# High words of queries and keys by ScalarE casts in place of transfers, in a clustered attention with two MLPs

## The chip, the cores and the metric

The kernel runs on one core of a Trainium2 chip. The metric is the device time of one execution in microseconds. Engines are named as in the profile: TensorE (PE, with PEld for its weight loads), VectorE (DVE), ScalarE (ACT), GpSimd (POOL) and SyncE (SP), whose queue issues nearly all the transfers (DMAs).

## The reference

Each query and each key is assigned to the nearest of 16 centroids of its head, and a query attends only to keys of its own cluster. The result goes through two MLPs, the second of them gated.

```python
batch, n_heads, seq, head_dim = (2, 8, 768, 64)          # 16 heads in all
q_assign = np.argmax(np.einsum('bhsd,hcd->bhsc', q_n, c_n), axis=-1)
k_assign = np.argmax(np.einsum('bhsd,hcd->bhsc', k_n, c_n), axis=-1)
mask = q_assign[:, :, :, None] == k_assign[:, :, None, :]
scores = np.where(mask, scale * np.matmul(q, k.transpose(0, 1, 3, 2)), -1000000000.0)
attn = np.exp(scores - np.max(scores, axis=-1, keepdims=True))
attn = attn / (np.sum(attn, axis=-1, keepdims=True) + 1e-09)
x = np.matmul(attn, v)          # then (1536, 512) rows
h = x @ w_in                    # 512 x 2048
x = (h * (1.0 / (1.0 + np.exp(-1.702 * h)))) @ w_out
g = x @ w_gate                  # 512 x 1536
out = (g * (1.0 / (1.0 + np.exp(-g))) * (x @ w_val)) @ w_out2
```

## The kernel before

**Attention** goes head by head (h = 0 to 15). A head has two stages on TensorE. In the *scores* stage twelve steps (six blocks of keys times two halves of 384 queries) each issue two matmuls into a bank `st` of PSUM (L707; three banks in turn), and beside each step one matmul `smax` of the *next* head (L657), whose maximum VectorE takes (`nm`, L662). ScalarE turns each `st` into exponentials `p` (L717). In the *values* stage TensorE multiplies `p` by v (`pv`) and sums of `p` by ones (`ps`, both L739); ScalarE needs no scores there, and does what is prepared for later heads.

**Low and high words.** TensorE reads 32-bit words in a rounded form, so queries and keys are split in a high word (rounded) and a low word (the rest). `q2` and `k2` of a head have 128 partitions and two planes: plane 0 of q2 has the high queries in rows 0 to 63 and the low ones in rows 64 to 127, plane 0 of k2 the low keys and then the high keys; plane 1 has the high words in rows 0 to 63, then 16 rows of the cluster and the row of maxima. For heads 8 to 15 the raw queries and keys lie together in one of four staging tiles `st` (q in rows 0 to 63, k in rows 64 to 127; `load_qk`, L428). `hi_staged` (L461) casts the whole of it into plane 0 of q2; so the high keys stand for a while where the low queries belong. `spread_hi` has three transfers (L468): the high keys from there to both planes of k2, and the high queries to plane 1 of q2. `lo_staged` (L465, VectorE) subtracts the high words from the staging tile, in place, and `spread_lo` (two transfers, L468 too) puts the low words in q2 and k2.

**Similarities.** At the end of the scores of an odd head h, `similar` computes the similarities to the centroids of heads h + 3 and h + 4 (`sims`, L572, eight matmuls), which need the high and low words of both; VectorE turns them into assignments (`largest`, then `assign` in the next, even head: `T`, `mx`, `oT`, two casts on ScalarE and two transfers from `oT`, L642 and L644). `mrow` (L689, after the first values) and the cast L691 make the row of maxima of head h + 1.

**Decoding.** The MLPs' weights arrive as 64-bit numbers. A piece is fetched raw (L265), ScalarE takes it apart (`a`, L280 and `t`, L283), VectorE joins it (L286, then L291 to `wo`), and it is stored (`keep`, L300 or L302). Six pieces are decoded in attention; `takes` says at which head and which block c of the values each part is done: part 0 is ScalarE's, parts 1 and 2 are VectorE's. Pool `dec` has one tile for each of `a` and `t`.

**The end of attention and the MLPs** are ordered by a planner (`Plan`): tasks with an estimated time, dependencies and a latest start taken from TensorE's order, which is fixed by the order in which tasks are made. The last head's scores are tasks of that plan, between the first products of the MLP. `late_from` says from which tile on a ring (a set of tiles used in turn) lies in memory that attention held.

Each engine and the SP queue run their instructions in order: an instruction that waits holds all behind it.

Of the kernel before, what the change touches and what calls it, by code (L numbers as in the profile page):

```python
# [184 lines left out]
def tile_cluster_attention_two_mlps(ctx: ExitStack, tc: tile.TileContext, qk, v, cen, w1, w2, wg, wv, w3, out):  # L185
    nc = tc.nc
# [16 lines left out]
    def pool(stack, name, bufs, **kw):  # L203
        return stack.enter_context(tc.tile_pool(name=name, bufs=bufs, reuse_waits="tile", **kw))
# [5 lines left out]
    xc_p = [pool(ctx, "xc0", X0)]  # L210
    xf_p = [pool(ctx, "xf0", 1)]
    raw_p = pool(ctx, "raw", RAW - 1)
    dec_p = pool(ctx, "dec", 1)
    wo_p = pool(ctx, "wo", 1)
    r_p = [pool(ctx, "r0", 1)]
    scr_p = pool(ctx, "scr", 1, space=DRAM)
    ps_m = pool(ctx, "ps_m", 1, space=PSUM)
# [241 lines left out]
    def hi_staged(h):  # L459

        nc.scalar.copy(q2(h)[:, 0, :], stage[h % NST])  # L461

    def lo_staged(h):
        t = stage[h % NST]
        nc.vector.tensor_tensor(out=t.bitcast(F32R), in0=t, in1=q2(h)[:, 0, :].bitcast(F32), op=ALU.subtract)  # L465

    def bits(to, of):
        nc.sync.dma_start(out=to.bitcast(F32), in_=of.bitcast(F32))  # L468

    def spread_hi(h):  # L470
        bits(k2(h)[D:2 * D, 0, :], q2(h)[D:2 * D, 0, :])
        bits(k2(h)[0:D, 1, :], q2(h)[D:2 * D, 0, :])
        bits(q2(h)[0:D, 1, :], q2(h)[0:D, 0, :])

    def spread_lo(h):
        bits(q2(h)[D:2 * D, 0, :], stage[h % NST][0:D])
# [375 lines left out]

    takes = {}
    for h in range(5, 5 + EARLY_ITEMS, 2):
        takes.update({(h, 0): (0,), (h, 1): (1, 2), (h, 3): (0,), (h, 5): (1,), (h + 1, 4): (2,)})
    sims = similar([0])
    keep_warm(18)
    hi_k(1)
# [145 lines left out]
    for h in range(NH):  # L1004
# [11 lines left out]
        if h == NH - 1:  # L1016
            moved_sums(h - 1)
            send_sums(h - 1)
        if h > 2:
            moved(h - 1)  # L1020
            if h % 2 and 4 < h < NH - 1:
                load_sums((h - 3) // 2)
# [9 lines left out]
        if 1 < h < NH - 1:  # L1032
            mneg(h + 1)
            if h % 2 and ahead and h > 3:
                do(largest([h + 3, h + 4], similar([h + 3, h + 4], ps_s, "s")))
            for part in takes.get((h, 0), ()):
                take(part)
            values(h, 0)
            values(h, 1)
            mrow(h + 1)  # L1040
        if h > 1 and h + 2 < NH:
            load_v(h + 2)
        if h + 6 < NH and h > 1:
            load_qk(h + 6)
        casts = [] if not h else [h + 4] if h < 3 else [7, 8] if h == 3 else [h + 5] if h + 5 < NH else []
        if h > 3 and casts:
            hi_staged(casts[0])
        elif casts and h != 1:
            hi_q(casts[0])
            hi_k(casts[0])  # L1050
        elif casts:
            hi_q(casts[0])
# [13 lines left out]
        for c in range(SC) if more else ():  # L1066
            if h > 1:
                if c > 1:
                    values(h, c)
                beside_block(h, c)  # L1070
            elif h or c:
                pv(h, c)
            if c == 0:
                if h < 2:
                    load_v(h + 1)
                    if h:
                        load_v(h + 2)
                        hi_k(casts[0])
                    for i in casts:
                        lo_q(i, nc.gpsimd)  # L1080
                        lo_k(i, nc.gpsimd)
                    load_qk(h + 6)
                if ahead:
                    if h + 5 == NH:
                        close_slot(FIRST)
                        close_slot("st")
                        xs_p.append(right("xs", 2))
                        xc_p.append(right("xc1", XC - X0 - 1))
            if h == 0:
# [12 lines left out]
            if h == 1:  # L1102
                beside(2, c, ((ps_m, "m"), (ps_s, "s")))
                if c == 3:
                    mneg(2)
                    sims = similar([4], ps_s, "s")
                    mrow(2)
                if c == 4:
                    do(largest([4, 5], sims + similar([5], ps_s, "s")))
            for part in takes.get((h, c), ()) if c else ():  # L1110
                take(part)
            for i in casts[-1:] if h > 2 else ():
                for at, step in ((2, spread_hi), (2, lo_staged), (5, spread_lo)):
                    if c == at and h > 3:
                        step(i)
            if h in (2, 3) and c == 1:
                lo_q(casts[0])
                lo_k(casts[0])
            for n in beside_values.get((h, c), ()):
                next(more_steps[n], None)  # L1120
            if h == 1 and c == 4:
                fetch_to(2)
            if h == 3 and c == 4:
                do(largest([6, 7], similar([6, 7], ps_s, "s")))
                hi_staged(8)
                spread_hi(8)
            if h == 4 and c == 1:
                lo_staged(8)
                spread_lo(8)
            if h == 3 and c in (3, 4):  # L1130
                to_x(0, c - 3)
# [9 lines left out]
    def after_attention():  # L1141
        close_slot((NH - 1) % NQK)
        slot_stack["c"].close()
        att.close()
        late_pools.update(
            {n: pool(ctx, f"{n}_late", bufs) for n, bufs in (
                ("c", CB // 2), ("e", EB - 1), ("wd", WO), ("g", GB), ("xc", 1), ("sp", 3), ("b0", 1), ("w", 1), ("raw", 1), ("dec", 1), ("wo", 1),
            )},
            a=pool(ctx, "ps_a", 1, space=PSUM),
        )  # L1150
# [14 lines left out]
    a_tile, t_tile, wo_tile = (in_turn((lambda pl=pl: pl, 1), (lambda n=n: late(n), 1)) for pl, n in ((dec_p, "dec"), (dec_p, "dec"), (wo_p, "wo")))  # L1165
    rings = {
        "raw": p.ring(RAW, lambda: raw_tile([128, 512, 2], I32, "raw")),
        "a": p.ring(2, lambda: a_tile([128, 512], F32, "a")), "t": p.ring(2, lambda: t_tile([128, 512], I32, "t")),
        "wo": p.ring(2, lambda: wo_tile([128, 512], F32, "wo")),
        "wd": p.ring(WO, late_tile("wd", [128, 512], F32, "wd")),  # L1170
        "w": p.ring(WB, new_wf, held["w"]),
        "s": p.ring(1, new_s, held["s"]),
        "b0": p.ring(2, lambda: new_block(0), held["b0"]),
# [16 lines left out]
    late_from.update({"a": 1, "t": 1, "wo": 1, "raw": RAW - 1, "w": WB - 1, "b0": 1, "xc": XC - 1, "c": CB // 2, "p1": 1, "u2": 1, "u3": 1})  # L1190

    kept = {}

# [389 lines left out]
    def last_values():  # L1583
        for c in range(SC):
            p.task(
                "PE", (2 + 2 * (c in SUMS)) * (2 * HALF / 2.4 + 5), lambda c=c: values(NH - 1, c), (), (),
                exp_tasks[2 * c:2 * c + 2] + [t for a in SUMS.get(c, ()) for t in adds[a]],
            )
            yield

# [3 lines left out]
    next(more)  # L1594
    next(first)
    next(more)
    last_adds()
    slots = last_values()
    for k in range(2):
# [10 lines left out]

    def plan_norm(hp, first):
        if hp > NH // 2 - 3:
            if first:
                first = [p.task("SP", 1000, lambda: send_sums(NH - 1), (), (), first)]
            got = p.task("SP", 1000, lambda: load_sums(hp), (), (), first)
            turned = p.task("DVE", 350, lambda: invert(hp), (), (), [got])
            first = [p.task("SP", 1000, lambda: (send_recips(hp), load_recips(hp)), (), (), [turned, *norms[:-1]])]
        norms.append(p.task(
            "POOL", 1850, lambda: norm_pair(hp), (), [(last_x, (hp % (H // 2), t0)) for t0, _ in parts], first,
        ))  # L1620
        return norms[-1]

# [79 lines left out]
```

## Time and profile before

| | |
|---|---|
| median of 3 runs | 788.19 us (787.99 to 788.4) |
| the profiled execution | 790.38 us, span 788.6 us |
| granted TensorE clock, mean | 0.993 |
| PE busy | 773.5 us (98%) |
| DVE busy | 667.4 us (85%) |
| ACT busy | 485.4 us (62%) |
| POOL busy | 126.7 us (16%) |

All times in the rows are microseconds from the span's start, unless they say ns. Attention takes about the first 260 us, the two MLPs the rest. A busy TensorE is not one at its full clock: the granted clock is read beside it (1.00 is 2.4 GHz, 0.50 is 1.2 GHz). In rows of a timeline, the bracket at the end is the idle time of the engine ahead of the instruction, and what ended it.

### The profile page before, as it was taken

To read this page: it belongs to the slowest core of one execution; us is meant where nothing else is said; L and a number is where in the kernel's file an instruction comes from. 1 tells how busy PE (TensorE), PEld (TensorE's weight loads), DVE (VectorE), ACT (ScalarE), POOL (GpSimd) and SP (SyncE) were. 2 spreads that over 40 slices of the span, in tenths; PEclk is the share of its full clock that TensorE was granted. 3 is DMA by queue.
4 is the path that set the end of the run, shared out by engine and by line. 5 is a ranking of instruction groups with operands and counts; after the bars stand their busy time and mean duration, and the time that the engine had idled before them with its cause. 6 is when DMAs were issued, how large, how long until landed. Compare 5 with 4: busy or idle time off the path is not lost.

```text
span 788.6 us, 11966 instructions
## 1 busy us (share of the span) xinstructions
PE 773.5 (98%) x4238; PEld 662.6 (84%) x4238; DVE 667.4 (85%) x1220; ACT 485.4 (62%) x851; POOL 126.7 (16%) x136
## 2 busy tenths in 40 slices
PE   8999998989999999999999999999999999999998
PEld 6995766567575899999999999999999999999996
DVE  7887878879895899999799889999988998877752
ACT  7758656558576786787487767667453654534332
POOL 8564334335355000000000000000000000000000
PEclk9999999999999999999999999999999999999999
DMA  5132466555124477663166784647423222322102
GB/s 124 38 100 58 101 175 164 150 143 141 24 61 133 176 245 239 205 200 134 41 221 233 239 276 151 227 163 243 161 92 105 81 65 97 115 72 73 63 1 80
DMA packets 54427, 106.66 MB, mean 135 GB/s; under 512 B 19984, under 2 KB 25472, under 8 KB 54368
## 3 DMA queue, kind: packets, MB, share of 16 engines
q1 hardware_dynamic: 54144, 105.58, 43.1%
q8 instruction: 33, 0.54, 0.3%
q10 hardware_dynamic: 224, 0.33, 0.1%
q14 instruction: 26, 0.21, 0.1%
HBM read 76.23 MB, written 21.06 MB: 123 GB/s over the span
## 4 chain that ended last, share of the span: by engine, by line
PE 87%; DVE 8%; DMA 2%; issue 1%; ACT 1%; SPq 0%; DVEq 0%; ACTq 0%
PE h L384 36%; PE a L384 29%; PE pv L739 7%; PE st L707 6%; PE ps L739 3%; PE smax L657 3%; DVE nm L662 3%; PE pv L807 2%; DMA k<-st 1%; DMA k<-q 1%; PE sims L572 1%; DVE b L379 1%; PE warm L492 0%; DVE s L1246 0%; DVE wo L291 0%
## 5 line engine op out<-in xcount | busy, mean ns | idle before, releaser
L384 PE MATMUL h<-xc,b 128*128 128x384 f32 x1680 | 316.8, 337 | 0.1
L384 PEld LDWEIGHTS h<-xc,b 128*128 128x128 f32 x1680 | 291.7, 188 | 10.4 <-DVE u L1302 2.3
L384 PE MATMUL a<-g,sp 128*128 128x512 f32 (+1 forms) x768 | 144.3, 336 | 0.0
L384 PEld LDWEIGHTS a<-g,sp 128*128 128x128 f32 x768 | 124.9, 188 | 16.9
L384 PE MATMUL a<-sp,g 128*128 128x512 f32 x432 | 109.6, 393 | 0.0
L662 DVE TENSOR_REDUCE nm<-smax 128x1 f32<-128x384 f32 x192 | 98.6, 555 | 12.5 <-PE smax L657 12.0
L717 ACT ACTIVATE p<-st 128x384 f32<-128x384 f32 x192 | 88.5, 491 | 30.8 <-PE st L707 25.8
L726 POOL TENSOR_TENSOR add<-p 128x384 f32<-128x384 f32 x84 | 84.8, 1030 | 114.5 <-ACT p L717 112.9
L707 PE MATMUL st<-q,k 128*128 128x384 f32 (+1 forms) x384 | 97.9, 345 | 0.8 <-ACT p L717 0.8
L384 PEld LDWEIGHTS a<-sp,g 128*128 128x128 f32 x432 | 80.1, 187 | 13.2
L376 ACT CAST b<-s 128x512 fp32r<-128x512 f32 x80 | 49.5, 620 | 55.1 <-PE h L384 47.7
L707 PEld LDWEIGHTS st<-q,k 128*128 128x128 f32 (+1 forms) x384 | 68.2, 190 | 10.8 <-issue 7.2
L1302 DVE TENSOR_TENSOR u<-h,p 128x384 f32<-128x384 f32 x80 | 44.2, 553 | 30.3 <-PE h L384 30.1
L739 PE MATMUL pv<-p,v 128*64 128x384 f32 x336 | 69.2, 522 | 0.0
L657 PE MATMUL smax<-k,q 80*128 80x384 f32 x192 | 63.0, 345 | 1.2 <-DVE nm L662 0.8
L280 ACT ACTIVATE a<-raw 128x512 f32<-128x512 f32 x68 | 45.7, 672 | 23.0 <-DVE wo L291 10.6
L379 DVE TENSOR_TENSOR b<-s,b 128x512 fp32r<-128x512 f32 x80 | 54.7, 685 | 1.6 <-ACT b L376 0.4
L379 DVE TENSOR_TENSOR g<-c,g 128x768 fp32r<-128x768 f32 x56 | 52.6, 953 | 1.5 <-ACT g L376 0.9
L376 ACT CAST g<-c 128x768 fp32r<-128x768 f32 x56 | 45.3, 834 | 12.3 <-DVE c L1317 11.8
L286 DVE SCALAR_TENSOR_TENSOR t<-a,t 128x512 int32<-128x512 int32 x68 | 46.1, 683 | 3.9 <-ACT t L283 3.9
L376 ACT CAST b<-w 128x768 fp32r<-128x768 f32 x35 | 29.2, 834 | 29.7 <-PE h L384 29.7
L1310 ACT ACTIVATE c<-c 128x384 f32<-128x384 f32 (+1 forms) x56 | 38.3, 684 | 14.3 <-DVE c L1302 13.5
(141 smaller groups left out, 885.0 us busy)
## 6 DMA issues: line engine op xcount, KB each, us to landing
raw<-in_w SPq DMA_DIRECT2D x44, 512.0 KB, 3.9
w<-scr SPq DMA_DIRECT2D x30, 512.0 KB, 4.2
raw<-in_wg SPq DMA_DIRECT2D x12, 512.0 KB
raw<-in_wv SPq DMA_DIRECT2D x12, 512.0 KB, 3.9
w<-scrg SPq DMA_DIRECT2D x12, 512.0 KB, 4.0
w<-scrv SPq DMA_DIRECT2D x12, 512.0 KB, 3.5
st<-in_qk SPq DMA_DIRECT2D x31, 192.0 KB, 3.6
scr<-wd SPq DMA_DIRECT2D x23, 256.0 KB, 5.5
```

Source lines behind the costliest of these rows:

```text
L280: nc.scalar.activation(a, raw[:, :, 1].bitcast(F32), ACTF.Copy, scale=2.0**-112)
L286: nc.vector.scalar_tensor_tensor(out=t, in0=a.bitcast(I32), scalar=3, in1=t, op0=ALU.logical_shift_left, op1=ALU.bitwise_or)
L376: nc.scalar.copy(to, of)
L379: eng.tensor_tensor(out=to, in0=of, in1=hi.bitcast(F32), op=ALU.subtract)
L384: nc.tensor.matmul(out=out_ps, lhsT=lhs[a], rhs=rhs[b], start=(start and j == 0), stop=(stop and j == 2), skip_group_check=True, **kw)
L657: nc.tensor.matmul(out=ps, lhsT=q2(h)[0:ONE + NC, 1, c * 128:(c + 1) * 128], rhs=k2(h)[0:ONE + NC, 1, n * HALF:(n + 1) * HALF],)
L662: nc.vector.tensor_reduce(out=nm_t[h][:, c, n:n + 1], in_=ps, axis=AX.X, op=ALU.max)
L707: nc.tensor.matmul(out=ps, lhsT=k2(h)[0:rows, a, c * 128:(c + 1) * 128], rhs=q2(h)[0:rows, a, at], start=(a == 0), stop=(a == 1),)
L717: nc.scalar.activation(p_t[h, c][:, n * HALF:(n + 1) * HALF], ps, ACTF.Exp, scale=scale)
L726: nc.gpsimd.tensor_tensor(out=add_t[h, c][:, at], in0=p_t[h, c][:, at], in1=p_t[h, c + 1][:, at], op=ALU.add)
L739: nc.tensor.matmul(out=ps[n * D:(n + 1) * D, 0:HALF], lhsT=w, rhs=x[:, n * HALF:(n + 1) * HALF], start=start, stop=stop, skip_group_check= ...
L1302: lambda: nc.vector.tensor_tensor(out=to.tile[:, part], in0=ps.tile[:, 0:HALF], in1=other.tile, op=ALU.add),
```

## The change

1. `spread_hi` and its three transfers are gone. `hi_others` has three casts on ScalarE that take the high words straight from the staging tile: the high keys to both planes of k2, the high queries to plane 1 of q2.
2. `hi_staged` comes ahead of the values of a head, before the row of maxima; `hi_others` behind that row. `lo_staged` comes at block 1 of the values, `spread_lo` at block 2 (before: blocks 2 and 5). The fetches of v and of the next queries and keys come behind `spread_lo`; they stood ahead of the values' blocks.
3. The decoding parts move: in odd heads part 0 of the first piece from the start of the values to block 2, of the second to block 4; VectorE's parts behind `lo_staged`.
4. Pools `dec` and `wo` have two tiles from the start; before, the second lay in memory freed by attention.
5. In the last head, the copy of head 14's output (`moved`) becomes a task of the plan, and the sums of heads 12 and 13 are fetched at the head's start.

```diff
-    dec_p = pool(ctx, "dec", 1)
-    wo_p = pool(ctx, "wo", 1)
+    dec_p = pool(ctx, "dec", 2)
+    wo_p = pool(ctx, "wo", 2)
...
+    def hi_others(h):
+        nc.scalar.copy(k2(h)[D:2 * D, 0, :], stage[h % NST][D:2 * D])
+        nc.scalar.copy(k2(h)[0:D, 1, :], stage[h % NST][D:2 * D])
+        nc.scalar.copy(q2(h)[0:D, 1, :], stage[h % NST][0:D])
...
-    def spread_hi(h):
-        bits(k2(h)[D:2 * D, 0, :], q2(h)[D:2 * D, 0, :])
-        bits(k2(h)[0:D, 1, :], q2(h)[D:2 * D, 0, :])
-        bits(q2(h)[0:D, 1, :], q2(h)[0:D, 0, :])
...
-        takes.update({(h, 0): (0,), (h, 1): (1, 2), (h, 3): (0,), (h, 5): (1,), (h + 1, 4): (2,)})
+        takes.update({(h, 2): (0,), (h, 3): (1,), (h, 4): (0,), (h, 5): (2,), (h + 1, 3): (1, 2)})
...
         if h == NH - 1:
             moved_sums(h - 1)
             send_sums(h - 1)
-        if h > 2:
+            load_sums((h - 3) // 2)
+        elif h > 2:
             moved(h - 1)
...
-            for part in takes.get((h, 0), ()):
-                take(part)
+            if h > 3 and h + 5 < NH:
+                hi_staged(h + 5)
             values(h, 0)
             values(h, 1)
             mrow(h + 1)
-        if h > 1 and h + 2 < NH:
-            load_v(h + 2)
-        if h + 6 < NH and h > 1:
-            load_qk(h + 6)
...
         if h > 3 and casts:
-            hi_staged(casts[0])
+            hi_others(casts[0])
...
+            for i in casts[-1:] if h > 3 else ():
+                for at, step in ((1, lo_staged), (2, spread_lo)):
+                    if c == at:
+                        step(i)
+            if h > 1 and c == 2:
+                if h + 2 < NH:
+                    load_v(h + 2)
+                if h + 6 < NH:
+                    load_qk(h + 6)
+            for part in takes.get((h, c), ()):
                 take(part)
-            for i in casts[-1:] if h > 2 else ():
-                for at, step in ((2, spread_hi), (2, lo_staged), (5, spread_lo)):
-                    if c == at and h > 3:
-                        step(i)
...
-                spread_hi(8)
+                hi_others(8)
...
-    late_from.update({"a": 1, "t": 1, "wo": 1, "raw": RAW - 1, ...
+    late_from.update({"raw": RAW - 1, ...
...
+    moves = p.task("ACT", 2 * act(HALF), lambda: moved(NH - 2), (), ())
```

TensorE's instructions stand in the same order in both kernels. ScalarE, from the copy of the output at the end of the scores of head 5 (`xf<-pv`) to the first exponentials of head 6, before:

```order
L766 COPY xf<-pv 64x384 x2
L280 ACTIVATE a<-raw 128x512
L283 ACTIVATE t<-raw 128x512
L691 CAST row<-mrow 6x128
L461 CAST q_0_165<-st_196 128x768
L280 ACTIVATE a<-raw 128x512
L283 ACTIVATE t<-raw 128x512
L717 ACTIVATE p<-st 128x384 x5
```

And after:

```order
L766 COPY xf<-pv 64x384 x2
L461 CAST q_0_165<-st_196 128x768
L691 CAST row<-mrow 6x128
L464 CAST k_0_166<-st_196 64x768
L465 CAST k_0_166<-st_196 64x768
L466 CAST q_0_165<-st_196 64x768
L280 ACTIVATE a<-raw 128x512
L283 ACTIVATE t<-raw 128x512
L280 ACTIVATE a<-raw 128x512
L283 ACTIVATE t<-raw 128x512
L717 ACTIVATE p<-st 128x384 x5
```

The first cast now stands ahead of the row of maxima, three more behind it, and both decoding pairs behind these.

The SP queue in head 6, from the transfer of the row of maxima to the low words of head 11 (q_1, k_1), before:

```order
L692 DMA q_2_180<-row 1x6x128
L436 DMA v_192<-in_v 128x6x64
L428 DMA st_194<-in_qk 64x768 x2
L644 DMA q_4_170<-oT 16x768
L644 DMA k_4_171<-oT 16x768
L793 DMA r<-recips 64x768 x2
L468 DMA k_1_189<-q_1_188 64x768 x2
L468 DMA q_1_188<-q_1_188 64x768
L300 DMA scr_95<-wo 128x256 x2
L468 DMA q_1_188<-st_197 64x768
L468 DMA k_1_189<-st_197 64x768
```

And after, to the store of the decoded piece:

```order
L692 DMA q_2_180<-row 1x6x128
L644 DMA q_4_170<-oT 16x768
L644 DMA k_4_171<-oT 16x768
L793 DMA r<-recips 64x768 x2
L473 DMA q_1_188<-st_197 64x768
L473 DMA k_1_189<-st_197 64x768
L436 DMA v_192<-in_v 128x6x64
L428 DMA st_194<-in_qk 64x768 x2
L300 DMA scr_95<-wo 128x256 x2
```

The three transfers of high words are gone, and the low words passed the fetches and the store.

ScalarE at the start of the last head, where the sums of head 14 are copied (`sums<-ps`); a piece of the difference:

```order
 L769 COPY sums<-ps 65x384
-L766 COPY xf<-pv 64x384 x2
 L717 ACTIVATE p<-st 128x384 x6
-L1323 COPY p_3031<-h 128x384
+L766 COPY xf<-pv 64x384 x2
+L1322 COPY p_3038<-h 128x384
```

The copy of the output went from ahead of six exponentials to behind them.

## Rows read from the trace of the kernel before

**Rows 1.** Windows from values to values: length; PE, PEld, DVE, ACT, POOL busy; PEclk, DMA, GB/s.

```profile
88.83:119.87 31.04, 29.11 (x157) 19.24 (x158) 25.12 (x47) 19.72 (x41) 11.87 (x13) 0.95 0.63 161
119.87:150.95 31.08, 29.07 (x156) 19.20 (x158) 25.74 (x48) 19.72 (x41) 11.84 (x13) 0.95 0.64 165
150.95:198.07 47.12, 44.03 (x238) 29.45 (x239) 39.24 (x73) 31.25 (x63) 19.71 (x20) 0.96 0.54 134
198.07:210.89 12.82, 12.82 (x75) 8.80 (x77) 11.55 (x21) 6.60 (x15) 3.99 (x5) 1.00 0.08 18
```

**Rows 2.** Windows after the wait in head 7, and in the MLPs.

```profile
137.00:138.00 1.00, 1.00 (x6) 0.27 (x4) 0.93 (x3) 0.00 (x0) 0.00 (x0) 0.50 0.76 307
...
259.00:768.00 509.00, 508.90 (x2784) 472.49 (x2783) 450.43 (x795) 307.58 (x510) 1.84 (x1) 1.00 0.45 150
```

**Rows 3.** Timeline of TensorE: start, length, what [idle ahead, what ended it].

```profile
135.34 0.58 PE L572 MATMUL sims<-q,cs 128*128 128x384 f32 x2 [1.95 <-DMA q<-st]
...
190.94 0.45 PE L657 MATMUL smax<-k,q 80*128 80x384 f32 x1 [0.32 <-DVE nm L662]
...
195.32 0.34 PE L657 MATMUL smax<-k,q 80*128 80x384 f32 x1
195.49 0.52 PE L572 MATMUL sims<-q,cs 128*128 128x384 f32 x2
...
244.82 1.39 PE L707 MATMUL st<-q,k 128*128 128x384 f32 x6 [0.77 <-ACT p L717]
```

**Rows 4.** The chain that ended last, in head 7: start, length, what.

```profile
127.84 4.38 DMA k<-q
132.29 0.48 SPq L468
132.82 3.12 DMA k<-st
```

**Rows 5.** Timeline of ScalarE, from the end of head 7's scores.

```profile
132.93 0.95 ACT L766 COPY xf<-pv 64x384 f32<-64x384 f32 x2
133.90 0.67 ACT L280 ACTIVATE a<-raw 128x512 f32<-128x512 f32 x1
134.48 0.64 ACT L283 ACTIVATE t<-raw 128x512 int32<-128x512 uint32 x1
139.70 0.25 ACT L691 CAST row<-mrow 6x128 fp32r<-6x128 f32 x1 [4.58 <-PE mrow L689]
```

**Rows 6.** Timeline of ScalarE in the values of head 6.

```profile
121.50 0.25 ACT L691 CAST row<-mrow 6x128 fp32r<-6x128 f32 x1 [0.30 <-PE mrow L689]
121.66 0.82 ACT L461 CAST q<-st 128x768 fp32r<-128x768 f32 x1
123.95 0.83 ACT L642 CAST q<-oT 16x768 fp32r<-16x768 f32 x1 [1.47 <-DVE oT L630]
124.79 0.83 ACT L642 CAST k<-oT 16x768 fp32r<-16x768 f32 x1
126.71 0.49 ACT L717 ACTIVATE p<-st 128x384 f32<-128x384 f32 x1 [1.09 <-PE st L707]
```

**Rows 7.** Timeline of VectorE: the twelve maxima of heads 7 and 11.

```profile
126.89 6.38 DVE L662 TENSOR_REDUCE nm<-smax 128x1 f32<-128x384 f32 x12 [1.39 <-PE smax L657]
...
190.33 5.91 DVE L662 TENSOR_REDUCE nm<-smax 128x1 f32<-128x384 f32 x12
```

**Rows 8.** Groups by line over the span: times | busy us, mean ns | idle.

```profile
L286 DVE SCALAR_TENSOR_TENSOR t<-a,t 128x512 int32<-128x512 int32 x68 | 46.1, 683 | 3.9 <-ACT t L283 3.9
...
L465 DVE TENSOR_TENSOR st<-st,q 128x768 fp32r<-128x768 f32 x8 | 7.6, 956 | 0.1
...
L445 ACT CAST k<-st 64x768 fp32r<-64x768 f32 x7 | 5.8, 832 | 0.2
...
L785 DVE RECIPROCAL rc<-rc 128x12 f32<-128x12 f32 x7 | 1.6, 228 | 0.2
```

More of the change, by code (lines that the diff above doesn't have):

```diff
@@ L1109, in tile_cluster_attention_two_mlps @@
                     do(largest([4, 5], sims + similar([5], ps_s, "s")))
-            for part in takes.get((h, c), ()) if c else ():
+            for i in casts[-1:] if h > 3 else ():
[8 more added lines that the diff above has]
+            for part in takes.get((h, c), ()):
                 take(part)
-            for i in casts[-1:] if h > 2 else ():
-                for at, step in ((2, spread_hi), (2, lo_staged), (5, spread_lo)):
-                    if c == at and h > 3:
-                        step(i)
             if h in (2, 3) and c == 1:
@@ L1146, in after_attention @@
             {n: pool(ctx, f"{n}_late", bufs) for n, bufs in (
-                ("c", CB // 2), ("e", EB - 1), ("wd", WO), ("g", GB), ("xc", 1), ("sp", 3), ("b0", 1), ("w", 1), ("raw", 1), ("dec", 1), ("wo", 1),
+                ("c", CB // 2), ("e", EB - 1), ("wd", WO), ("g", GB), ("xc", 1), ("sp", 3), ("b0", 1), ("w", 1), ("raw", 1),
             )},
@@ L1164, in tile_cluster_attention_two_mlps @@
     raw_tile = in_turn((lambda: raw_p, RAW - 1), (lambda: late("raw"), 1))
-    a_tile, t_tile, wo_tile = (in_turn((lambda pl=pl: pl, 1), (lambda n=n: late(n), 1)) for pl, n in ((dec_p, "dec"), (dec_p, "dec"), (wo_p, "wo")))
     rings = {
         "raw": p.ring(RAW, lambda: raw_tile([128, 512, 2], I32, "raw")),
-        "a": p.ring(2, lambda: a_tile([128, 512], F32, "a")), "t": p.ring(2, lambda: t_tile([128, 512], I32, "t")),
-        "wo": p.ring(2, lambda: wo_tile([128, 512], F32, "wo")),
-        "wd": p.ring(WO, late_tile("wd", [128, 512], F32, "wd")),
+        "a": p.ring(2, new_a), "t": p.ring(2, new_t), "wo": p.ring(2, new_wo), "wd": p.ring(WO, late_tile("wd", [128, 512], F32, "wd")),
         "w": p.ring(WB, new_wf, held["w"]),
@@ L1189, in tile_cluster_attention_two_mlps @@
     late_from = {n: 0 for n in ["wd", "g", "sp"] + [f"acc{i}" for i in range(6)]}
-    late_from.update({"a": 1, "t": 1, "wo": 1, "raw": RAW - 1, "w": WB - 1, "b0": 1, "xc": XC - 1, "c": CB // 2, "p1": 1, "u2": 1, "u3": 1})
+    late_from.update({"raw": RAW - 1, "w": WB - 1, "b0": 1, "xc": XC - 1, "c": CB // 2, "p1": 1, "u2": 1, "u3": 1})
     kept = {}
@@ L1586, in last_values @@
                 "PE", (2 + 2 * (c in SUMS)) * (2 * HALF / 2.4 + 5), lambda c=c: values(NH - 1, c), (), (),
-                exp_tasks[2 * c:2 * c + 2] + [t for a in SUMS.get(c, ()) for t in adds[a]],
+                exp_tasks[2 * c:2 * c + 2] + [t for a in SUMS.get(c, ()) for t in adds[a]] + [moves],
             )
@@ L1612, in plan_norm @@
         if hp > NH // 2 - 3:
-            if first:
+            if hp == NH // 2 - 1:
                 first = [p.task("SP", 1000, lambda: send_sums(NH - 1), (), (), first)]
-            got = p.task("SP", 1000, lambda: load_sums(hp), (), (), first)
-            turned = p.task("DVE", 350, lambda: invert(hp), (), (), [got])
+                first = [p.task("SP", 1000, lambda: load_sums(hp), (), (), first)]
+            turned = p.task("DVE", 350, lambda: invert(hp), (), (), first)
             first = [p.task("SP", 1000, lambda: (send_recips(hp), load_recips(hp)), (), (), [turned, *norms[:-1]])]
         norms.append(p.task(
-            "POOL", 1850, lambda: norm_pair(hp), (), [(last_x, (hp % (H // 2), t0)) for t0, _ in parts], first,
+            "POOL", 1850, lambda: norm_pair(hp), (), [(last_x, (hp % (H // 2), t0)) for t0, _ in parts], [*first, moves],
         ))
```

## The prediction

> **What bounds the kernel now.** I read the windows first, then TensorE's timeline, then the chain of waits, then ScalarE and VectorE beside it. From 259 us on, TensorE is busy 508.90 of 509 us at the full clock [rows 2]: the two MLPs leave nothing to win, and the order of TensorE's instructions is the same in both kernels, so the change can act only in attention. There the undisturbed pace is known: a head without similarities takes 12.82 us, in which TensorE is busy 12.82 [rows 1]. Every odd head also runs eight matmuls of similarities; a matmul starts 0.17 after the one before it (the two rows at 195 in [rows 3]), so they add 8 x 0.175 = 1.4. A pair of heads should take 2 x 12.82 + 1.4 = 27.04. It takes 31.04 (heads 4 and 5) and 31.08 (6 and 7), and heads 8 to 10 take 47.12 where 3 x 12.82 + 2 x 1.4 = 41.26 would do [rows 1]. The excess is 4.00 + 4.04 + 5.86 = **13.9 us**, and that is the prize.
>
> Its cause stands in the chain [rows 4]. At the end of an odd head TensorE waits 1.95 us for the low words of the last head (at 135.34 in [rows 3]; there are three of this kind, and a shorter one at 196.7). Those words go into rows 64 to 127 of q2, from which the high words of the keys are first copied away by two transfers. So SP's queue holds the low transfer back until the high ones have landed (4.38 from issue), then spends 0.48 issuing q and 3.12 until k lands. After each of the three long waits TensorE works on at half clock: a microsecond in that stretch shows it busy 1.00 with a granted clock of 0.50, its lower level of 1.2 GHz (137 to 138 us in [rows 2]). This half of the loss is not in the idle time at all.
>
> The Trainium skill (Trainium Kernel Development and Optimization, Best Practices) says that matmul busy time is no measure of the distance to the limit. The trace agrees: 137 to 138 shows a busy engine at half its pace, and by idle time alone the three long waits, about 2 us each, would put the prize near 6 us.
>
> **The change part by part.** *The transfers of high words go*, 3 for each of 8 heads, and with them the wait between high and low. Three casts on ScalarE take their place. One such cast of 64 x 768 takes 0.832 [rows 8], so 2.5 us a head and 24 x 0.832 = 20.0 us in all. Nothing of that costs time if it lies under the values (the stage after the scores, where TensorE needs no exponentials). That has to be checked in an even and in an odd head.
>
> Even head (number 6, values from 119.87): ScalarE is done with the head before at 121.50 - 0.30 = 121.20 [rows 6]. Now follow the first cast 0.82 to 122.02, the row of maxima 0.25 to 122.27, three casts 2.5 to 124.8, the two casts of the assignment 1.7 to 126.5. The exponentials start at 126.71 after an idle 1.09. The cover holds with 0.2 to spare.
>
> Odd head (number 7), without the stall: the similarities follow the last scores and the values start about 133.9. ScalarE is done with the head before at 132.93 + 0.95 = 133.88 [rows 5]; first cast to 134.7; the row must wait for some nine matmuls, about 135.6, and ends at 135.85; casts to 138.35; then two decoding pairs, each 134.48 + 0.64 - 133.90 = 1.22, to 140.8. The exponentials are wanted 126.71 - 119.87 = 6.84 after the start of the values, at 140.76. That is even. Three banks of scores let TensorE run about 0.5 ahead (one step of a score takes 0.53, twelve in 6.38 [rows 7]), so a delay under 0.5 costs nothing. If ScalarE comes out later, the loss is what exceeds that 0.5.
>
> The Trainium skill (ScalarE: Activation LUTs, What ACT_TABLE_LOAD costs) gives 186 ns + 0.833 ns an element with 93 ns of overlap between neighbours. The duration agrees (0.826 against 0.832). The overlap shows at 121.50 to 121.66 and between the decoding steps, but the two casts at 123.95 and 124.79 show none. With it the three casts take an estimated 2.3, ScalarE is done 0.2 sooner, and rival B below would have a chance of one in ten.
>
> *VectorE's steps are the same, in another order.* The low step (0.956 [rows 8]) now waits until the casts have read the staging tile, since it overwrites it: to 138.35 in the odd head. Behind it are queued a decoding step 0.683, two short ones below 0.23, another 0.683: done about 141.1. The first maximum was wanted 126.89 - 119.87 = 7.02 after the start of the values [rows 7], at 140.94. So it is 0.15 late, and up to 0.5 if VectorE itself comes later to the low step. Twelve maxima back to back take 5.91 instead of 6.38 [rows 7], so it is made up within the scores. In the even head: 124.8 + 0.96 + 2 x 0.69 = 127.1 against 126.89; same verdict. Bounds: nothing to 0.5 a head over seven heads; I take 0.9 in all.
>
> *Low words.* In the even head the low step ends at 125.8. SP then has q and k to issue; k starts about 126.9 behind the transfers of the assignment and the reciprocals, and lands 3.12 to 4.38 later [rows 4], 130.0 to 131.3. The second similarities want it at 135.34 - 1.95 = 133.39 [rows 3]. Two microseconds to spare: the four waits go, and with them the half clock. What is late next is ScalarE or VectorE, as above. The fetches of v and of the next queries and keys move behind the low words on SP; they start to move about 4.5 us before the next head's first cast wants them, against 3.12 to 4.38 for transfers of that size [rows 4], and that cast may come 0.9 late before the row of maxima suffers. Raw weights queue behind them; nobody waits for those within a head.
>
> *Head 10* stays bound by VectorE: TensorE loses 0.32 there (at 190.94 in [rows 3]), since an extra splitting step of the MLP's input stands behind the casts. ScalarE now comes 0.7 later to that split (2.5 of casts, less the 1.47 and 0.30 that it idles in an even head [rows 6]), so the loss grows by 0 to 0.7; I take 0.35. With the 0.32, which the prize counts, 0.67 stays.
>
> *The last head* sends six exponentials ahead of the copy of head 14's output. TensorE waited 0.77 for them (at 244.82 in [rows 3]); 0.95 of copying goes from ahead of them [rows 5], so the wait goes: 0.77. The sums come early, and the weights fetched behind them on SP some 5 us later; the blocks made from them are wanted some 10 us later, so at nothing; without that cover, up to 2 us.
>
> *Two decoding tiles* take one wait of ScalarE on VectorE out of the odd head, and let the MLPs' second decoding slot begin before attention ends. TensorE is full there: nothing.
>
> Sum: 13.9 + 0.77 - 0.32 - 0.35 - 0.9 = **13.1**. The profiled execution lasted 790.38 us, 1.8 more than its span of 788.6; it would become 777.3. The median of the three runs is 788.19, 2.2 below the profiled one: **775.1 us**.
>
> **The rivals.** **A**, the forecast: stalls gone, TensorE bound at its pace, 775.1 (788.19 - 13.9 - 0.77 = 773.5 if nothing is lost).
> **B**: ScalarE or VectorE becomes the bound. For it: an odd head leaves ScalarE no margin, and VectorE is busy 25.74 of a pair [rows 1] that is to take 27.04. Against it: 0.5 of tolerance at each head. Price: 0.4 to 0.8 more in each of seven heads, 2.8 to 5.6, taken from the forecast: 777.9 to 780.7, about 778.5.
> **C**: the low words still come last in some heads, because the fetches and reciprocals share the queue and the low step waits for the casts. For it: 4.38 from issue to landing has been seen. Against it: two microseconds of margin. Two of the stalls back at 4.0 each: 783.1.
> **D**, the slower side: the casts are not covered. All 20.0 us lie on ScalarE ahead of exponentials; if TensorE waits for all of them, 788.19 + 20.0 - 14.7 = 793.5. It decides once about 2.0 of the 2.5 us a head are uncovered, that is when ScalarE's free time in the values is under 0.5. Against it: an even head has 1.09 + 1.47 idle [rows 6], and the odd one 4.58 ahead of the row [rows 5], of which 2 are the stall and 1 the half clock.
> **E**: the change does not do what it says: another transfer holds the low words just as long. Only the 0.77 stays: 787.4. Against it: rows 4 name the transfer.
>
> **How the numbers follow.** A 0.62, B 0.24, C 0.05, D 0.04, E 0.05. About 0.2% (1.6 us) is what a measurement of this kernel can tell from no change. Faster: A, B and C, 0.91; same: E, 0.05; slower: D, 0.04. The range takes in A with all its bounds and most of B: 773.2 to 779.2.
>
> **What would show it.** Right: no wait of TensorE for q<-st or k<-st over 0.5 at the end of heads 5, 7 and 9, granted clock 1.00 from 100 to 180 us, pairs of heads at 27 to 27.5, first exponentials of a head within 0.5 of the score, and the wait at the last head's second scores gone. B shows as waits of TensorE for p or nm in every head at full clock; C as waits for q<-st with the clock falling; D as heads of over 15 us without similarities. The forecast is wrong above all if these small waits add up, or bring the half clock back.

## The result, and the profile after

The changed kernel takes 778.26 us (median of 4 runs, 777.22 to 778.64) beside 788.3 of the kernel before on the same chip (787.99 to 791.29): a ratio of 0.986, 95% interval 0.984 to 0.989. In a second series it took 777.49 beside 790.13 (0.985, 0.983 to 0.987). The forecast was 775.1, range 773.2 to 779.2: the sign and the range hold, the middle is 2.4 to 3.2 us too low. The profiled execution of the changed kernel lasted 778.64 us, its span 776.9.

Windows of the changed kernel, cut at the same places as [rows 1] (start of the values of heads 4, 6 and 8, to that of head 11), then the stretch from 100 to 180 us and the MLPs. Columns as in [rows 1]. Beside a wait or a window, a head's number stands for the time from the start of its values to the start of the next head's; `h` in code is the program's head.

```profile
89.99:117.24 27.25, 27.25 (x157) 18.93 (x158) 24.28 (x46) 24.66 (x47) 11.88 (x13) 1.00 0.45 109
117.24:144.50 27.26, 27.26 (x156) 18.96 (x158) 25.26 (x48) 24.55 (x47) 11.86 (x13) 1.00 0.61 145
144.50:186.91 42.41, 41.96 (x237) 28.98 (x239) 39.12 (x74) 38.38 (x72) 19.21 (x20) 1.00 0.52 127
100.00:180.00 80.00, 80.00 (x454) 55.03 (x453) 73.33 (x136) 72.68 (x137) 34.35 (x35) 1.00 0.55 136
259.00:768.00 509.00, 508.93 (x2771) 471.24 (x2770) 445.26 (x786) 300.19 (x497) 2.21 (x1) 1.00 0.44 148
```

The pairs take 27.25 and 27.26 where they took 31.04 and 31.08 [rows 1], the three heads 42.41 where they took 47.12. From 100 to 180 us TensorE stands busy all the time at the full clock. ScalarE has 4.9 us more in a pair (24.66 against 19.72): the copies.

TensorE's timeline after, the only wait over 0.2 us between 90 us and the end; its counterpart is the row at 190.94 in [rows 3].

```profile
180.81 0.45 PE L657 MATMUL smax<-k,q 80*128 80x384 f32 x1 [0.45 <-DVE nm L662]
```

ScalarE's timeline after, in the values of heads 6 and 7, to be laid beside [rows 6] and [rows 5].

```profile
118.60 0.83 ACT L461 CAST q<-st 128x768 fp32r<-128x768 f32 x1
119.45 0.25 ACT L691 CAST row<-mrow 6x128 fp32r<-6x128 f32 x1
119.73 0.83 ACT L464 CAST k<-st 64x768 fp32r<-64x768 f32 x1
120.57 0.83 ACT L465 CAST k<-st 64x768 fp32r<-64x768 f32 x1
121.42 0.83 ACT L466 CAST q<-st 64x768 fp32r<-64x768 f32 x1
122.27 0.83 ACT L642 CAST q<-oT 16x768 fp32r<-16x768 f32 x1
123.11 0.83 ACT L642 CAST k<-oT 16x768 fp32r<-16x768 f32 x1
124.14 0.49 ACT L717 ACTIVATE p<-st 128x384 f32<-128x384 f32 x1 [0.20 <-PE st L707]
...
132.73 0.83 ACT L461 CAST q<-st 128x768 fp32r<-128x768 f32 x1 [1.25 <-DMA st<-in_qk]
...
138.59 2.61 ACT L717 ACTIVATE p<-st 128x384 f32<-128x384 f32 x5
```

In the even head ScalarE goes without a pause from the first cast to the last and then waits 0.20 for the first score. In the odd head the first cast is late, since its fetch now stands behind the low words, and ScalarE goes from the second decoding pair straight into the exponentials.

The SP queue after, beside the times of issue in [rows 4]: both transfers of the low words are issued at 123.90 and 124.50, ahead of the fetches and of the decoded piece.

```profile
123.90 0.55 SPq L473 DMA_DIRECT2D q<-st  x1
124.50 0.59 SPq L473 DMA_DIRECT2D k<-st  x1
125.13 0.61 SPq L436 DMA_DIRECT2D v<-in_v  x1
```

### The profile page after: what moved, and what is told of

It is laid out like the page before. It is cut to its first block, busy times and chain, and to the rows that moved or that the text cites. A ratio compares the mean times of both kernels' runs of the same rounds, so it can differ in the third digit from the quotient of the medians.

```text
span 776.9 us, 11963 instructions
## 1 busy us (share of the span) xinstructions
PE 769.1 (99%) x4238; PEld 662.6 (85%) x4238; DVE 665.6 (86%) x1220; ACT 504.6 (65%) x875; POOL 126.6 (16%) x136
## 4 chain that ended last, share of the span: by engine, by line
PE 92%; DVE 5%; ACT 1%; issue 1%; POOL 1%; DMA 0%; POOLq 0%; DVEq 0%; ACTq 0%
PE h L384 36%; PE a L384 29%; PE st L707 8%; PE pv L739 7%; PE smax L657 4%; PE ps L739 3%; PE pv L807 2%; PE sims L572 2%; DVE nm L662 1%; PE warm L492 1%; DVE b L379 0%; DMA w<-scr 0%; DVE u L1301 0%; PE mrow L689 0%; DVE wo L291 0%
## 5 line engine op out<-in xcount | busy, mean ns | idle before, releaser
L739 PE MATMUL pv<-p,v 128*64 128x384 f32 x336 | 65.2, 495 | 0.0
```

What stands on the lines that cost most here:

```text
L739: nc.tensor.matmul(out=ps[n * D:(n + 1) * D, 0:HALF], lhsT=w, rhs=x[:, n * HALF:(n + 1) * HALF], start=start, stop=stop, skip_group_check= ...
```

## The experiments

### The same two kernels again, in more runs

Both kernels, unchanged, to see what spread each has by itself.

> The kernel before, once more, to see how its executions differ among themselves. Theory S: the three long waits of TensorE bring the half clock in a number of cases that differs from execution to execution, each costing 1.7 us; then the mean granted clock of an execution is 0.993 with three of them (790.4 us, the profiled one) and higher where there are fewer, at about 788 or 786.5. Rival: the clock is 0.993 in every execution, and the 2.2 us between the profiled execution and the others lie elsewhere, such as in the first 20 us.

> The changed kernel, once more. No long wait is left in it, so theory S expects a clock of 0.999 to 1.000 in every execution and a spread of about 1.5 us that comes from the first 10 us (there the first transfer landed 0.36 us later than in the profile of before, and TensorE's transposition of the centroids started 0.8 us later). Rival: the later start of that transposition belongs to the change; then it shows at about 5.7 us in every profile of the changed order and at 4.9 us in every one of the order before.

Measured: the kernel before 790.5 us in 12 runs, 786.39 to 792.91; the changed one 777.49, 777.42 to 778.77. With the runs of before that stood beside the experiments there are 55 runs with their mean granted clock:

```
clock   runs   median us   lowest to highest
0.991     9     791.8      791.1 to 792.9
0.993    19     790.3      788.7 to 791.8
0.994    11     790.4      789.9 to 791.3
0.995     6     788.7      788.4 to 790.7
0.996     5     788.8      787.7 to 789.9
0.998     5     786.7      786.4 to 787.5
```

The time lost to the lower level is what the clock is short of 1 times the span: 7.1 us at 0.991, 1.6 at 0.998, a difference of 5.5, and the medians differ by 5.1. So the stretches at half clock are not the same in every run of the kernel before; its time says how much of them it had. The changed kernel's clock is 0.999 or 1.0 in all four runs, and their spread is a fifth of that of the twelve.

### The copies alone, in the place of the transfers

```diff
-        bits(k2(h)[D:2 * D, 0, :], q2(h)[D:2 * D, 0, :])
-        bits(k2(h)[0:D, 1, :], q2(h)[D:2 * D, 0, :])
-        bits(q2(h)[0:D, 1, :], q2(h)[0:D, 0, :])
+        nc.scalar.copy(k2(h)[D:2 * D, 0, :], stage[h % NST][D:2 * D])
+        nc.scalar.copy(k2(h)[0:D, 1, :], stage[h % NST][D:2 * D])
+        nc.scalar.copy(q2(h)[0:D, 1, :], stage[h % NST][0:D])
```

(in the kernel before, inside `spread_hi`; nothing is moved)

> The kernel before with one part of the change alone: the three transfers of high words are replaced by three ScalarE casts at the same place, and nothing is moved. Theory W (the low words wait on the queue for the high words to land): with no high transfer the low words leave some 3 us sooner, behind the store of the decoded piece, and land at about the time they are wanted; the three long waits fall under 0.5 us. VectorE's low step then stands behind the casts and the decoding in odd heads, which costs some 0.7 us in each: 777 to 781, 8 to 11 below before. Rival P (the place of the low words on the queue decides): waits of over 1.5 us stay, with the half clock, 785 or more.

Measured: 792.3 us (ratio 1.004, 1.002 to 1.005), a little slower than before, far from the 777 to 781 expected and not by the rival's reason either. The waits for low words are gone: none stands in TensorE's timeline. In their place are these, ScalarE's row first and TensorE's behind it, in head 6:

```profile
123.39 0.83 ACT L471 CAST k<-st 64x768 fp32r<-64x768 f32 x1
124.23 0.83 ACT L472 CAST k<-st 64x768 fp32r<-64x768 f32 x1
125.08 0.83 ACT L473 CAST q<-st 64x768 fp32r<-64x768 f32 x1
...
126.35 0.62 PE L707 MATMUL st<-q,k 128*128 128x384 f32 x2 [0.69 <-ACT p L717]
128.02 0.45 PE L657 MATMUL smax<-k,q 80*128 80x384 f32 x1 [1.05 <-DVE nm L662]
...
129.00:130.00 1.00, 1.00 (x5) 1.00 (x4) 0.83 (x2) 1.00 (x3) 0.32 (x1) 0.50 0.71 184
```

The three copies stand behind the casts of the assignment, which wait for VectorE, and ahead of the exponentials; the first exponential comes at 125.81. The low step on VectorE waits for the third copy and holds the maxima. TensorE waits for both, and a stretch at half clock follows. Two such waits stand in each of the even heads 4, 6, 8 and 10, 7.3 us in all, and none in the odd ones. Taking the transfers away was right about the wait it removed and worth nothing by itself: the wait went to ScalarE.

### The new order with the transfers kept

```diff
-        nc.scalar.copy(k2(h)[D:2 * D, 0, :], stage[h % NST][D:2 * D])
-        nc.scalar.copy(k2(h)[0:D, 1, :], stage[h % NST][D:2 * D])
-        nc.scalar.copy(q2(h)[0:D, 1, :], stage[h % NST][0:D])
+        bits(k2(h)[D:2 * D, 0, :], q2(h)[D:2 * D, 0, :])
+        bits(k2(h)[0:D, 1, :], q2(h)[D:2 * D, 0, :])
+        bits(q2(h)[0:D, 1, :], q2(h)[0:D, 0, :])
```

(in the changed kernel, inside `hi_others`)

> The changed kernel with the three transfers back in place of the casts, issued where the casts stood; the new order, the two decoding tiles and the last head stay. Theory W: the high transfers are issued right behind the row of maxima, 5 us sooner than before, land about 4.4 us later, and the low words follow some 1 to 2 us ahead of the similarities that want them; the long waits go without the casts, and ScalarE keeps 2.5 us a head: 776 to 779, within 1 us of the changed kernel. Rival: without the casts the low words are held back again and the waits stay, 785 or more.

Measured: 778.0 us (ratio 0.986, 0.983 to 0.988), as the changed kernel. The transfers of the high words stand where the changed kernel has its copies, so in head 6 they leave at 119.63, and the low ones, though they still wait for them, at 124.25 (132.29 in [rows 4]). SP's rows:

```profile
119.63 1.17 SPq L473 DMA_DIRECT2D k<-q  x2
120.85 0.59 SPq L473 DMA_DIRECT2D q<-q  x1
...
124.25 0.49 SPq L473 DMA_DIRECT2D q<-st  x1
124.78 0.60 SPq L473 DMA_DIRECT2D k<-st  x1
```

Two shorter waits stay in head 8 and at its end, 1.20 us for the row of maxima and 0.41 for k's low words; the granted clock is 1.00 behind both. One of the four runs took 779.87 us at a clock of 0.997: with the transfers kept, a little of the lower level can come back, which no run of the changed kernel shows.

### The copies early, SP's queue in the old order

```diff
-                for at, step in ((1, lo_staged), (2, spread_lo)):
+                for at, step in ((2, lo_staged), (5, spread_lo)):
```

(in the changed kernel; the fetches and the decoding parts go back to their old places too)

> The changed kernel with the SyncE queue put back to its old order: the transfers of the low words, the fetches and the decoding stand where they stood before the change, and only the cast of the staging tile and the three copies of the high words keep their new, earlier place on ScalarE. Against the kernel with the copies at the old place (792.3 us) it differs in the place of the copies alone, as far as the attention stages go. Theory C (the copies failed there only because they stood between the casts of the similarities and the exponentials, 2.5 us on a ScalarE that had nothing to spare): with the copies early, no wait of TensorE over 0.7 us after 90 us, granted clock 0.998 or more, 777 to 780 us. Rival Q (the old order of the queue holds the low words by itself, behind fetches and decoding): a wait for the low words (q<-st or k<-st) of 1 us or more at the ends of the odd heads, half clock behind it, 784 us or more.

Measured: 777.88 us (0.986, 0.984 to 0.988); two pairs, cut here from the values of head 5 to those of heads 7 and 9, take 27.24 and 27.26 at clock 1.00. The second:

```profile
130.40:157.66 27.26, 27.26 (x156) 18.89 (x155) 25.08 (x48) 24.68 (x47) 11.92 (x13) 1.00 0.54 150
```

The low words leave at 125.13 and 125.68 and are in time. Head 10 loses 1.06, above the 0.7 allowed, where the changed kernel loses 0.45. This kernel keeps the two decoding tiles and the last head's edit of the changed kernel, which the kernel at 792.3 lacks; they are measured below. So the gain comes without the end of the transfers (the run before) and without the new order of the queue (this one); early transfers in a queue of the old order were not run. What the kernels that gain have in common, and the two that don't lack, is the place of the step that spreads the high words, by copies or by transfers: straight behind the cast of the staging tile and the row of maxima, and no longer at block 2 of the values, behind the assignment's casts (on ScalarE) or the fetches and its transfers (on SP). From there the chain of cast, high words, low step and low words ends in time by either road. All three kernels that gain also cast the staging tile ahead of the row of maxima; that step alone was not run, but at the old place it was not what held the copies: there, in head 6, that cast was over at 120.24 and the first copy began at 123.39.

### Filling the waits

```diff
-            for at, (i, n) in enumerate(todo):
+            for at, (i, n) in enumerate(todo * (1 + again * (h == hs[0]))):
+                at %= len(todo)
```

(in the kernel before; `again` is 3 where `h` is 5, 7 and 9, so TensorE repeats the first similarity there)

> The kernel before with work that is thrown away: at the three places of the long waits TensorE does the matmuls of the first similarity four times in place of once, some 2.1 us more at each, into the same bank, ahead of the matmul that waits for the low words. Nothing that the kernel waits for is earlier, and 36 matmuls are added. Theory I (the half clock follows from TensorE's standing still): the waits of 1.7 to 2.1 us are filled, the granted clock stays near 1.00 from 100 to 180 us, and what the half clock cost beyond the waits themselves comes back: of the 13.9 us of the three pairs some 6.1 are waits and 7.8 the rest, so 783 to 786 us, 4 to 7 below the 790.1 of the kernel before. Rival J (the half clock has another reason, or the rest of the loss is not the clock): 789 to 793 us, clock 0.991 to 0.995 as before.

Measured: 786.3 us (0.995, 0.994 to 0.997): 36 matmuls more, and 4.0 us less, just outside the 783 to 786 expected. All ten runs have a granted clock of 0.999 or 1.0. Windows of two pairs, from the values of head 5 to those of heads 7 and 9, which took 31.26 and 31.63 in the kernel before:

```profile
105.49:135.37 29.88, 29.68 (x168) 21.03 (x167) 24.94 (x47) 19.78 (x40) 11.88 (x12) 1.00 0.66 179
135.37:164.85 29.48, 29.43 (x168) 21.07 (x167) 25.30 (x47) 19.73 (x40) 11.87 (x12) 1.00 0.64 171
```

The low words come no earlier, and TensorE's work behind the wait starts at 105.49 as it did at 105.37 without the filling; only the clock is different. So the lower level followed from standing still. Its price is smaller than the 7.8 us expected, which was the prize less the three waits: 4.0 in these runs, and 5.5 by the mean clock of the profiled execution (0.007 of 788.6).

### Twice the copies

```diff
             hi_others(casts[0])
+            hi_others(casts[0])
```

> The changed kernel with the three copies of the high words made twice in heads 4 to 10: three more copies of 0.84 us, 2.5 us of ScalarE a head, in the same place; nothing else changes. Theory M (the even-head and odd-head walks of the prediction: ScalarE is done 0.2 to 0.5 us ahead of the first score): 2.0 to 2.3 us a head come through to TensorE, 14 to 16 us over seven heads, 790 to 795 us, and the wait stands at the first scores and smax, with half clock behind some of them. Rival N (ScalarE has more cover than the walks give, since exponentials can run behind the scores by some banks): under 783 us.

Measured: 804.34 us (1.020, 1.016 to 1.024), well above the 790 to 795 expected. TensorE's waits, in an even head (4) and an odd one (5):

```profile
98.16 0.63 PE L657 MATMUL smax<-k,q 80*128 80x384 f32 x1 [2.52 <-ACT k L642]
...
117.03 0.44 PE L707 MATMUL st<-q,k 128*128 128x384 f32 x1 [1.63 <-ACT p L717]
```

The even heads let all 2.52 us through: the first maxima of the next head want the cast of the assignment (L642), and ScalarE's margin is nothing. The odd ones let 1.63 through, a margin of 0.9. Four of the one, three of the other and 0.47 in head 10 make 15.5 us of waits, 15.0 more than the changed kernel has and inside the 14 to 16 expected. The half clock, which the expectation named and did not count, is nearly all of the rest: at a clock of 0.989 the span of 799.8 lost 8.8 us, and 15.0 + 8.8 = 23.8 of the 24.2 by which the profiled execution (801.58 us) stands above that of the changed kernel (777.42).

### The third copy on GpSimd

```diff
-        nc.scalar.copy(q2(h)[0:D, 1, :], stage[h % NST][0:D])
+        nc.gpsimd.tensor_copy(q2(h)[0:D, 1, :], stage[h % NST][0:D])
```

> The changed kernel with the third copy of the high words (queries, to the second plane) on GpSimd in place of ScalarE. It is wanted only in a later head. Theory M: odd heads lose 0.2 us each and head 10 0.45 us because ScalarE comes late by as much; with 0.84 us less on it these go, 776 to 777.5 us, 0.5 to 1.5 below the changed kernel. Rival G (GpSimd's copy takes several us and what stands behind it, or VectorE beside it, comes late): same or slower, 778 to 785 us.

Measured: 776.19 us, 776.04 to 776.37, below every run of the changed kernel: the best version here, 0.984 of before (0.981 to 0.986). Windows of two pairs, from the values of head 5 to those of heads 7 and 9:

```profile
102.94:130.00 27.06, 27.06 (x156) 19.02 (x155) 25.31 (x46) 22.93 (x44) 13.71 (x15) 1.00 0.60 146
130.00:157.03 27.03, 27.03 (x155) 18.99 (x154) 25.86 (x47) 23.06 (x44) 13.72 (x15) 1.00 0.61 153
```

The pairs reach the 27.04 that the prediction worked out as TensorE's pace, and head 10's wait is gone. The expectation put the 0.2 of a pair on the odd heads. The rows put it on the even ones, where the first matmul for the maxima (`smax`) comes late in the changed kernel (head 6, first three rows) and not here (last three):

```profile
123.43 0.62 PE L707 MATMUL st<-q,k 128*128 128x384 f32 x2
124.00 0.45 PE L657 MATMUL smax<-k,q 80*128 80x384 f32 x1
124.28 0.52 PE L707 MATMUL st<-q,k 128*128 128x384 f32 x2
...
122.04 0.62 PE L707 MATMUL st<-q,k 128*128 128x384 f32 x2
122.49 0.34 PE L657 MATMUL smax<-k,q 80*128 80x384 f32 x1
122.67 0.52 PE L707 MATMUL st<-q,k 128*128 128x384 f32 x2
```

From the first row to the third it is 0.85 there and 0.63 here. What that `smax` waits for is the second cast of the assignment on ScalarE, which ends at 123.94 there and at 121.98 here. GpSimd's copy takes 0.81 to 1.16 us where ScalarE's takes 0.83.

### One decoding tile

```diff
-    dec_p = pool(ctx, "dec", 2)
-    wo_p = pool(ctx, "wo", 2)
+    dec_p = pool(ctx, "dec", 1)
+    wo_p = pool(ctx, "wo", 1)
...
-        takes.update({(h, 2): (0,), (h, 3): (1,), (h, 4): (0,), (h, 5): (2,), (h + 1, 3): (1, 2)})
+        takes.update({(h, 2): (0,), (h, 3): (1, 2), (h, 4): (0,), (h + 1, 3): (1, 2)})
```

> The changed kernel with one tile each for decoded words and for written words in the attention stages in place of two; so that each part of decoding finds its tile free, two of them go together as before the change. Theory T0 (the prediction's price of nothing: decoding is off the path and its transfers are drained well before they are wanted): within 0.5 us of the changed kernel, 777 to 779 us, no new wait of TensorE over 0.3 us. Rival T1 (a second part of decoding waits for the first part's transfer, on ScalarE, ahead of the exponentials of an odd head): a wait of 1 us or more at first scores of odd heads, with half clock behind it, 782 us or more.

Measured: 780.6 us, 780.54 to 780.91, some 2.3 to 3.1 above the changed kernel, between the two theories' times. ScalarE in an odd head, and TensorE's wait for it:

```profile
108.29 0.67 ACT L283 ACTIVATE t<-raw 128x512 int32<-128x512 uint32 x1
110.50 0.67 ACT L280 ACTIVATE a<-raw 128x512 f32<-128x512 f32 x1 [1.54 <-DVE rc L784]
...
112.15 0.45 PE L707 MATMUL st<-q,k 128*128 128x384 f32 x1 [0.88 <-ACT p L717]
```

The second piece waits 1.54 for VectorE to be done with the tile, and three waits of 0.88, 0.72 and 0.72 come through, without half clock. It is rival T1's mechanism at a smaller size. The pool and the order of the decoding parts were changed together, so that what each is worth alone stays open.

### The last head as before

```diff
-            load_sums((h - 3) // 2)
-        elif h > 2:
+        if h > 2:
```

(in the changed kernel; the task for the copy of the output is taken out too)

> The changed kernel with the last head's edit undone: the loads of the sums and their move are again planned beside the last scores as before. Theory L (the term of the prediction): the 0.77 us wait of TensorE for an exponential in the last head is back and nothing else, so 778.2 to 779.5 us, 0.77 above the changed kernel (777.5 to 778.3). Rival L0 (the wait goes for another reason, as the attention ends 13 us earlier, or the move costs as much elsewhere): no such wait, 777.3 to 778.3 us.

Measured: 777.99 us, 777.9 to 778.69. The wait is back, as long as in [rows 3]:

```profile
232.32 0.62 PE L707 MATMUL st<-q,k 128*128 128x384 f32 x2 [0.77 <-ACT p L717]
```

The span is 776.2 beside 775.6 of the changed kernel's second profile. In the medians 0.5 of it shows beside the 777.49 of the second series, nothing beside the 778.26 of the first. The time lies below the 778.2 to 779.5 expected and in the rival's range, so it decides nothing; the wait is shown, its price only as the trace has it.

## Why the prediction was right, and where it was not

**The sum came out to 0.1 us, one of its terms for another reason than forecast; its base was wrong.** From the start of head 4's values to the long run of MLP matmuls took 170.25 us in the profiled execution before (88.83 to 259.08) and 157.03 after (89.99 to 247.02): 13.22 less, beside 13.1 forecast. The step that failed is the last of the sum, *the median of the three runs is 788.19, 2.2 below the profiled one: 775.1 us*. The 13.1 was made on an execution at clock 0.993, which lost some 5.5 us to the lower level. Executions near 788.2 lost less (in the table 0.995 to 0.996 go with 788.7 and 788.8, 3 to 4 us lost), and there was so much less to win; the clocks of the three runs themselves are not on record. Against its own execution the sum gave 777.3, and the medians came out at 777.49 and 778.26.

**The start was not in the sum.** In the profiled execution after, the first product of the centres comes at 5.69 us, in that of before at 4.92. In the second pair of profiles it is the other way round (5.69 before, 4.93 after). It comes with the run, and not with the change; head 4's values began 1.16 later. The two profiles of the changed kernel differ by it (spans 776.9 and 775.6). That the medians 778.26 and 777.49 differ by it too is likely and not shown: each series has runs near 777.4 and near 778.7.

TensorE's timeline of the changed kernel, first profile and second:

```profile
5.69 0.45 PE L541 MATMUL ctp<-ident,cn 128*128 128x128 f32 x1 [0.81 <-POOL v L514]
...
4.93 0.30 PE L541 MATMUL ctp<-ident,cn 128*128 128x128 f32 x1
```

**The prize and what is left of it.** Windows of 109.24 us [rows 1] became 96.92: 12.32 of 13.9. What stays is 1.58, beside 0.32 + 0.35 + 0.9 = 1.57 in the sum: 0.21 and 0.22 in the pairs, 1.15 in heads 8 to 10, of which the wait in head 10 is 0.45 (0.67 forecast). That the totals agree is in part luck. The 0.9 was put on VectorE, whose low step would hold the first maxima in even and odd heads. No odd head loses anything by that. What is lost instead is 0.20 to 0.22 in each of the even heads 4, 6, 8 and 10, at the `smax` that waits for ScalarE's cast of the assignment (its rows stand with the third copy on GpSimd, which takes this away); some 0.3 of the 1.15 are not traced. The last head gave its 0.77.

**The cause was named too narrowly.** *The transfers of high words go, 3 for each of 8 heads, and with them the wait between high and low*: that is what happened in the changed kernel, but the transfers need not go. With them the gain is the same; without them, at the old place, there is none. The late link was the start of the high words; whether early transfers gain in a queue of the old order too is open. The prediction had the times to see it: the cast ended at 122.48 [rows 6], the transfer of the high words in the chain began at 127.84 [rows 4], and those 5.4 us are longer than the 4.38 that it took.

**The walks of ScalarE.** Even head: 0.2 to spare in the forecast, 0.20 idle in the profile ahead of the exponentials. But the walk asked only what the exponentials want. The `smax` of the next head wants the cast of the assignment sooner; for it there was no margin, and doubled copies came through there in full. *The cover holds* was some 0.2 short in each even head. Odd head: *that is even* is what the trace shows; by the doubled copies it could bear 0.9, beside the 0.5 allowed; the late fetch (1.25 of waiting) is nearly hidden, since the row of maxima has to be waited for anyway. The price of the copies, taken without overlap, held too. The Trainium skill (ScalarE: Activation LUTs, What ACT_TABLE_LOAD costs) gives back-to-back ACTIVATEs about 93 ns of overlap; the three copies, casts in the trace, start 0.84 and 0.85 apart at 0.83 each, so the measurement decides here.

**Two decoding tiles: nothing** was wrong. The walk of the odd head laid two decoding pairs end to end, and that takes the second tile; without it, and with the parts joined, 2.3 to 3.1 us come back. The term was in the 13.1 without being priced.

**Rival B**, ScalarE or VectorE as the bound, gave 777.9 to 780.7, and the first median, 778.26, lies in it: the time alone does not tell A from B, and the range held partly because it was drawn to take in most of B. The trace tells them apart. B wanted 0.4 to 0.8 more in each of seven heads; ScalarE does bind, but by some 0.2 in four.

**Rival D**, copies that nothing covers, gave 793.5, and in the old place they cost 792.3. That the two are near is luck: D let all 20.0 us through, and the trace has 7.3 us of waits, in the even heads alone, and some 7.1 lost at the lower level (clock 0.991 over a span of 790.3). That the copies must be covered is shown; D's size is not.

**The half clock**: *this half of the loss is not in the idle time at all* holds, and that it follows from the idle time is shown. Its size is 4.0 to 5.5, not the 7.8 that the prize leaves beside the long waits. Some 2 us of the 13.9 are neither the three long waits nor the clock; 0.85 of them are the shorter waits of head 10, the rest stays open.

## What to carry to other kernels

When a transfer is late, look at where its chain begins before replacing a link: here an earlier start of one step was worth nearly all of it, by copies or by transfers. Put an added copy in an engine's queue ahead of whatever waits there for another engine; the same three copies stood in a kernel 1.4% faster in one place (with the second decoding tile and the last head's edit) and 0.4% slower in another. When checking that cover, ask of every instruction behind the copies who wants it first, not only of the last one. Make a sum against the execution it was read from, and if the granted clock differs between runs, compare the clock before subtracting from a median.

## What the runs showed of the hardware

Idle time of TensorE cost more than its own length: filling three waits with thrown-away matmuls made a kernel 4.0 us faster. Not every wait is followed by the lower level. Single waits of 1.20 and 1.06 us were followed by a clock of 1.00, and waits of 0.69 and 1.05 close together by 0.50. In the kernel with twice the copies the same wait, 2.5 us, was followed by 0.50 at 98 us and by 1.00 at 133 us:

```profile
99.00:100.00 1.00, 1.00 (x5) 1.00 (x4) 0.60 (x2) 0.49 (x1) 0.00 (x0) 0.50 0.49 104
...
135.00:136.00 1.00, 1.00 (x8) 1.00 (x7) 1.00 (x3) 0.96 (x3) 0.80 (x1) 1.00 0.72 172
```

VectorE's scaling of the centres (L536), ahead of their first product, took 0.91 us in one profile of the changed kernel and 0.49 in another, with the same memsets of GpSimd beside it; no run tells why.
